# Streaming attention and a wave mixer on one core: pools and woven generators against static tiles in one listed order, with turns by DMA

## The chip, the cores and the metric

The kernel runs on one core of a Trainium2 chip. The metric is the device time of one execution in microseconds (us), here the median of three runs. The profile is one execution of the same program; its span runs from the first to the last instruction and is a little shorter than the measured time. Engines: PE multiplies matrices and writes to PSUM, DVE and ACT are the two engines that read PSUM and do elementwise work (ACT also has the table functions exp and sine), POOL works on SBUF only and issues casting DMAs, SP issues plain DMAs. Each engine carries out its instructions in program order and waits on semaphores for the others, so the order in which the program lists the work is part of its speed.

## The reference, cut to what matters

```python
# attention: B=4, H=8 heads, S=768, D=64; heads 0, 2, 6 are "retrieval", the other five "streaming"
scores = (q @ k.T) / sqrt(D)
causal = rel >= 0                                   # rel = query position - key position
stream_keep = causal & ((key < 4) | (rel < 64))     # 4 sink keys and a window of 64
mask = causal for heads 0, 2, 6; stream_keep for heads 1, 3, 4, 5, 7
a = softmax(where(mask, scores, -1e9))
x = (a @ v) laid out as (B, S, 512)

# wave mixer on x: w_tok_* are (768, 768) over tokens, w_theta and w_ch (512, 512) over channels
theta = x @ w_theta
zr, zi = x * cos(theta), x * sin(theta)
y = w_tok_r @ zr + w_tok_i @ zi                     # over tokens, per batch
u = x + y
out = u + relu(u @ w_ch)
```

All inputs and the output are float32; both kernels compute in bf16 with float32 accumulation.

## The kernel before

Work is written as Python generators that yield an estimate of their PE cost; `weave` interleaves the next batch's attention with the mix of the batch at hand. Tiles come from pools: three PSUM pools of two slots each (`ps_s` of two banks, `ps_m` and `ps_x` of one).

```python
    ps_s = ctx.enter_context(tc.tile_pool(name="ps_s", bufs=2, space=bass.MemoryType.PSUM))
    ps_m = ctx.enter_context(tc.tile_pool(name="ps_m", bufs=2, space=bass.MemoryType.PSUM))
    ps_x = ctx.enter_context(tc.tile_pool(name="ps_x", bufs=2, space=bass.MemoryType.PSUM))
    # ... (cut)
    def load_qk(b, parts=((0, 8),)):          # casting DMAs on POOL's queue; the first batch in two parts
        # ... (cut)
                nc.gpsimd.dma_start(out=state[what, b][:, sl], in_=src[:, sl])

    def transposes(b, n):                     # n: one of four pairs of heads
        # ... 12 transposes of 64x128 into pt for q and for k ...
            if what == "q" and b > 0:
                nc.scalar.copy(o, i)          # qT
            else:
                nc.vector.tensor_copy(o, i)   # kT, and the first batch's qT
        sinks(n)                              # copies the 4 sink keys of streaming heads to kS (POOL)

    def score_unit(n, banks, un):
        # retrieval heads: 128 keys against all later queries, in rows of up to 512 columns
        # streaming heads: 12 blocks of 64 keys, each against its own 64 queries and the next 64:
                for c in range(NQ):
                    lo = max(64 * c if c != 1 else 0, q0)
                    hi = min(64 * c + 128, S, q0 + w)
                    if lo < hi:
                        half = slice(64 * (c % 2), 64 * (c % 2) + 64)
                        mms[y].append((ps[half, y, lo - q0:hi - q0], kT[n][rows, c * 64:(c + 1) * 64], qT[n][rows, lo:hi]))
        # ... (cut) exp on ACT into P or P_st, masks on DVE afterwards

    def sink_scores():                        # sink keys of all five streaming heads in one product
        # ... 6 matmuls (kS, qT), then exp into p_sink

    def values(b, i):                         # 128 queries, 4 heads at a time
        for par in range(2):
            # ...
                else:
                    s = STREAM.index(h)
                    if i:
                        mms.append((av[:, g], p_sink[:, i * 128:(i + 1) * 128], vs[:, b, s]))
                    mms.append((av[:, g], P_st[:, s, 256 * i + 64:256 * i + 192], vx[:, s, i]))
                    mms.append((av[:, g], P_st[:, s, 256 * i + 128:256 * i + 256], vt[:, h, i]))
            # ...
            nc.vector.reciprocal(r, av[:, :, D])      # the 65th column of v is 1, so it holds the sum
            nc.vector.tensor_tensor(dst, av[:, :, :D], r.unsqueeze(2).to_broadcast([128, 4, D]), ALU.mult)

    def turn_x(b, i):
        pt = ps_x.tile([128, 1024], BF16, tag="x", name="pt")
        for kk in range(KD):
            nc.tensor.transpose(pt[:, kk * 128:(kk + 1) * 128], x[:, i, kk * 128:(kk + 1) * 128], ident)
        nc.vector.tensor_copy(xT[:, :, i * 128:(i + 1) * 128], pt[:, :DM].rearrange("p (k t) -> p k t", k=KD))

    def phases(b, i):                         # theta for two blocks, then
        nc.scalar.activation(ct, ps, AF.Sin, bias=half_pi)
        nc.scalar.activation(st, ps, AF.Sin)
        for y in range(2):
            nc.vector.tensor_tensor(state["zr", b][:, i + y], x[:, i + y], ct[:, y], ALU.mult)
            nc.gpsimd.tensor_tensor(state["zi", b][:, i + y], x[:, i + y], st[:, y], ALU.mult)

    def mix(b):
        def turn(t):                          # as turn_x, for u; the copy to uT is on ACT
        def channel(t):                       # 4 matmuls with w_ch, relu and add on DVE, store on SP
        # per block t of 128 tokens: 12 matmuls into py, u = x + py on DVE
    # ... (cut)
    for b in range(B):
        if b + 1 < B:
            m = mix(b)
            if b == 0:
                m = chain(token_weights(2, NB), m)    # transposes of w_tok, by PE
            weave((m, 23000), (attention(b + 1), 19000))
        else:
            drain(mix(b))
```

Of the kernel before, what the change touches and what calls it, by code (L numbers as in the profile page):

```python
# [18 lines left out]
STREAM = [1, 3, 5, 7, 4]  # L19


def drain(gen):
    for _ in gen:
        pass


def weave(*parts):

    live = [[0.0, n, g, float(total)] for n, (g, total) in enumerate(parts)]
    while live:  # L30
        live.sort(key=lambda x: (x[0] / x[3], x[1]))
        part = live[0]
        try:
            part[0] += next(part[2])
        except StopIteration:
            live.pop(0)
# [3 lines left out]
def kernel(  # L40
    ctx: ExitStack,
    tc: tile.TileContext,
    q: bass.AP,
    k: bass.AP,
    v: bass.AP,
    is_retrieval: bass.AP,
    n_sink,
    window,
    moe_w_theta: bass.AP,
    moe_w_tok_r: bass.AP,  # L50
    moe_w_tok_i: bass.AP,
    moe_w_ch: bass.AP,
    out: bass.AP,
):
    nc = tc.nc
    B, H, S, D = q.shape
    DM = H * D
    NB = S // 128
    KD = DM // 128
    n_sink = int(n_sink)  # L60
    window = int(window)
    assert window == 64 and n_sink * len(STREAM) <= 32
    NS = n_sink * len(STREAM)
    scale = 1.0 / math.sqrt(D)

    const = ctx.enter_context(tc.tile_pool(name="const", bufs=1))
    big = ctx.enter_context(tc.tile_pool(name="big", bufs=1))
    two = ctx.enter_context(tc.tile_pool(name="two", bufs=2))
    stage = ctx.enter_context(tc.tile_pool(name="stage", bufs=4))
    work = ctx.enter_context(tc.tile_pool(name="work", bufs=2))  # L70
    ps_s = ctx.enter_context(tc.tile_pool(name="ps_s", bufs=2, space=bass.MemoryType.PSUM))
    ps_m = ctx.enter_context(tc.tile_pool(name="ps_m", bufs=2, space=bass.MemoryType.PSUM))
    ps_x = ctx.enter_context(tc.tile_pool(name="ps_x", bufs=2, space=bass.MemoryType.PSUM))

    ctx.enter_context(tc.manual_schedule())


    ident = const.tile([128, 128], BF16, name="ident")
    m_causal = const.tile([128, 128], BF16, name="m_causal")
    m_stream = const.tile([128, S], BF16, name="m_stream")  # L80
    half_pi = const.tile([128, 1], F32, name="half_pi")
    w_theta_sb = const.tile([128, KD, DM], BF16, name="w_theta_sb")
    w_ch_sb = const.tile([128, KD, DM], BF16, name="w_ch_sb")
    wtokT = [const.tile([128, NB, S], BF16, name=f"wtokT{n}") for n in "ri"]

    qT = [big.tile([128, S], BF16, name=f"qT{n}") for n in range(4)]
    kT = [big.tile([128, S], BF16, name=f"kT{n}") for n in range(4)]

    kS = [big.tile([128, 128], BF16, name=f"kS{n}") for n in range(4)]
    vt = big.tile([128, H, NB, D + 1], BF16, name="vt")  # L90

    vx = big.tile([128, len(STREAM), NB, D + 1], BF16, name="vx")

    vs = big.tile([128, B, len(STREAM), D + 1], BF16, name="vs")
    p_sink = big.tile([128, S], BF16, name="p_sink")

    NQ = S // 64
    P_st = big.tile([128, len(STREAM), NQ * 128 + 64], BF16, name="P_st")

    state = {}  # L100


    def load_v(b, pairs=range(4)):
        src = v[b].rearrange("h (j p) d -> p h j d", p=128)
        for n in pairs:
            t = stage.tile([128, 2, NB, D], F32, tag="st_v", name="st_v")
            state["v", b, n] = t
            for x, h in enumerate(PAIRS[n]):
                nc.sync.dma_start(out=t[:, x], in_=src[:, h])


    def load_qk(b, parts=((0, 8),)):
        for what in "qk":
            state[what, b] = two.tile([128, H, NB * D], BF16, tag=f"{what}b", name=f"{what}b")
        for hs in parts:
            for what, a in (("q", q), ("k", k)):
                src = a[b].rearrange("h (p j) d -> p h (j d)", p=128)
                sl = slice(*hs)
                nc.gpsimd.dma_start(out=state[what, b][:, sl], in_=src[:, sl])

    def cast_v(b, n, first=False):
        t = state["v", b, n]
        h0, h1 = PAIRS[n]
        (nc.vector if first else nc.gpsimd).tensor_copy(vt[:, h0:h1 + 1:2, :, :D], t)
        for x, h in enumerate((h0, h1)):
            if not IS_RETR[h]:
                s = STREAM.index(h)
                nc.gpsimd.tensor_copy(vx[:64, s, :, :D], t[:64, x])
                nc.gpsimd.tensor_copy(vx[64:, s, 1:, :D], t[64:, x, :NB - 1])

    def sinks(n):
        for x, h in enumerate(PAIRS[n]):
            if not IS_RETR[h]:
                c = STREAM.index(h) * n_sink
                rows = slice(64 * x, 64 * x + 64)
                nc.gpsimd.tensor_copy(kS[n][rows, c:c + n_sink], kT[n][rows, :n_sink])


    def transposes(b, n):
        h0, h1 = PAIRS[n]  # L140
        for what, dst in (("q", qT), ("k", kT)):
            pt = ps_x.tile([128, 1024], BF16, tag="x", name="pt")
            for j in range(NB):
                for x, h in enumerate((h0, h1)):
                    nc.tensor.transpose(pt[64 * x:64 * x + 64, j * 128:(j + 1) * 128], state[what, b][:, h, j * D:(j + 1) * D], ident)  # L145
            o = dst[n].rearrange("d (p j) -> d p j", j=NB)
            i = pt[:, :S].rearrange("d (j p) -> d p j", j=NB)
            if what == "q" and b > 0:
                nc.scalar.copy(o, i)
            else:  # L150
                nc.vector.tensor_copy(o, i)  # L151
        sinks(n)
# [3 lines left out]
    LOW = [[(0, 0, 512)], [(1, 128, 384), (3, 384, 128)], [(2, 256, 256)]]  # L156
    HIGH = [[(0, 512, 256), (1, 512, 256)], [(2, 512, 256), (3, 512, 256)], [(4, 512, 256), (5, 640, 128)]]


    def units(n, half):  # L160
        rs, w = (LOW, (0, 512)) if half == 0 else (HIGH, (512, 256))
        h0, h1 = PAIRS[n]
        if n == 0:
            return [(n, [(0, h0, r), (1, h1, r)]) for r in rs]
        if n == 1:
            return [(n, [(1, h1, rs[0]), (0, h0, w)]), (n, [(1, h1, rs[1]), (1, h1, rs[2])])]
        return [(n, [(0, h0, w), (1, h1, w)])]

    pending = []

    def masks_now():
        while pending:
            pending.pop(0)()

    def score_unit(n, banks, un):
        ps = ps_s.tile([128, 2, 512], F32, tag="s", name="ps")
        mms = [[], []]
        width = []
        used = [sum(w for _, _, w in what) for _, _, what in banks if isinstance(what, list)]
# [72 lines left out]
        if masks:  # L252
            pending.append(causal)
# [197 lines left out]
    at = 0  # L451
# [99 lines left out]
```

The softmax here doesn't subtract the row's maximum and nothing guards it: scores larger than these inputs give would overflow.

## Time and profile before

| | us |
|---|---|
| measured, median of 3 (lowest, highest) | 258.34 (257.64, 259.43) |
| span of the profiled execution | 255.5 |
| mean granted PE clock | 0.984 |

The costliest groups, by line and tile:

```profile
L336 POOL TENSOR_TENSOR zi<-x,st 128x512 bf16<-128x512 bf16 x24 | 30.0, 1268 | 104.9 <-ACT st L333 104.9
L349 ACT COPY uT<-pt 128x512 bf16<-128x512 bf16 x24 | 14.1, 586 | 46.7 <-PE pt L347 46.7
L327 PE MATMUL ps<-w_theta_sb,xT 128*128 128x512 bf16 x89 | 24.2, 391 | 7.9 <-DVE xT L318 7.6
L368 DVE TENSOR_TENSOR u<-x,py 128x512 bf16<-128x512 bf16 x24 | 16.5, 687 | 23.8 <-PE py L364 23.8
L356 DVE SCALAR_TENSOR_TENSOR ot<-pc,u 128x512 f32<-128x512 f32 x24 | 16.5, 689 | 8.5 <-PE pc L354 7.3
```

A line reads: source line, engine, operation, output <- inputs, shapes, count; then the busy time of the group and the mean in ns of one; then how long the engine stood idle just before the instructions of the group, and what ended most of that. Idle time of an engine that is not the limit costs nothing. PE's records overlap, since matmuls are pipelined: the time that a stream of matmuls needs is the distance between their starts, not the sum of their durations.

### The profile page before, as it was taken

What the parts mean: (1) busy time and instruction counts of PE and PEld (TensorE: products, weight loads), DVE (VectorE), ACT (ScalarE), POOL (GpSimd) and SP (SyncE); (2) the same over time, 40 slices, a digit from 0 to 9 for tenths busy, and PEclk for the clock granted to TensorE, in tenths of its full rate; (3) what the DMA queues carried; (4) which work ended last, traced back from release to release, by engine and by line L of the source; (5) the groups of instructions that cost most, each with busy time, mean ns of one, the idle gap of its engine ahead of it and who ended that gap; (6) DMA issues with size and microseconds to landing.
All of it is one profiled execution on the core that took longest, in us unless ns stands there. A gap on an engine that the chain in (4) does not pass through costs nothing.

```text
span 255.5 us, 5058 instructions
## 1 busy us (share of the span) xinstructions
PE 192.3 (75%) x2095; PEld 109.5 (43%) x2124; DVE 134.8 (53%) x312; ACT 111.0 (43%) x142; POOL 84.9 (33%) x133
## 2 busy tenths in 40 slices
PE   0202659774677999889798999876989998868993
PEld 0101436642463456544444456433444564324440
DVE  6103686766443547654656387445573874442433
ACT  2002327553548764244568721636697216341010
POOL 8532168018639300031687000216940002161000
PEclk9999999999779999999999999999999999999998
DMA  7999237998235891110356960030001100300123
GB/s 133 190 194 181 65 83 132 213 166 136 37 73 114 119 187 48 45 41 0 126 124 113 190 154 30 13 123 3 0 3 41 44 22 24 123 3 0 41 82 123
DMA packets 40006, 22.61 MB, mean 88 GB/s; under 512 B 26160, under 2 KB 36912, under 8 KB 39984
## 3 DMA queue, kind: packets, MB, share of 16 engines
q0 software_dynamic: 11440, 9.71, 24.8%
q1 hardware_dynamic: 28544, 12.59, 19.0%
q8 instruction: 16, 0.26, 0.5%
q14 instruction: 6, 0.05, 0.1%
HBM read 25.71 MB, written 6.29 MB: 125 GB/s over the span
## 4 chain that ended last, share of the span: by engine, by line
PE 47%; ACT 16%; DVE 13%; issue 11%; DMA 6%; POOL 4%; POOLq 1%; DVEq 0%; ACTq 0%
PE py L364 19%; PE ps L209 7%; PE pav L306 5%; ACT P L229 5%; DMA kb<-in_k_dram 5%; PE ps L327 4%; ACT ct L332 4%; PE pc L354 4%; DVE kT L151 3%; PE pt L145 3%; DVE zr L335 3%; DVE ot L356 2%; DVE x L310 2%; POOL zi L336 2%; PE ps L277 2%
## 5 line engine op out<-in xcount | busy, mean ns | idle before, releaser
L336 POOL TENSOR_TENSOR zi<-x,st 128x512 bf16<-128x512 bf16 x24 | 30.0, 1268 | 104.9 <-ACT st L333 104.9
L209 PE MATMUL ps<-qT,kT 64*64 64x128 bf16 (+6 forms) x380 | 25.6, 256 | 21.5 <-DVE kT L151 16.8
L364 PE MATMUL py<-zi,wtokTi 128*128 128x512 bf16 x137 | 37.8, 379 | 1.7 <-POOL zi L336 1.4
L364 PE MATMUL py<-zr,wtokTr 128*128 128x512 bf16 x130 | 36.6, 380 | 1.7 <-issue 0.8
L349 ACT COPY uT<-pt 128x512 bf16<-128x512 bf16 x24 | 14.1, 586 | 46.7 <-PE pt L347 46.7
L229 ACT ACTIVATE P<-ps 128x1024 bf16<-128x1024 f32 (+2 forms) x24 | 20.9, 919 | 23.5 <-PE ps L209 23.4
L335 DVE TENSOR_TENSOR zr<-x,ct 128x512 bf16<-128x512 bf16 x24 | 17.3, 763 | 25.9 <-ACT ct L332 25.9
L327 PE MATMUL ps<-w_theta_sb,xT 128*128 128x512 bf16 x89 | 24.2, 391 | 7.9 <-DVE xT L318 7.6
L368 DVE TENSOR_TENSOR u<-x,py 128x512 bf16<-128x512 bf16 x24 | 16.5, 687 | 23.8 <-PE py L364 23.8
L209 PEld LDWEIGHTS <-kT 64*64 64x64 bf16 (+1 forms) x380 | 12.7, 108 | 37.3 <-DVE kT L151 17.8
L332 ACT ACTIVATE ct<-ps,half_pi 128x1024 f32<-128x1024 f32 x12 | 13.4, 1114 | 25.7 <-PE ps L327 17.3
L354 PE MATMUL pc<-w_ch_sb,uT 128*128 128x512 bf16 x96 | 24.2, 379 | 0.0
L310 DVE TENSOR_TENSOR x<-pav,r 128x256 bf16<-128x256 f32 x48 | 20.4, 425 | 1.7
L356 DVE SCALAR_TENSOR_TENSOR ot<-pc,u 128x512 f32<-128x512 f32 x24 | 16.5, 689 | 8.5 <-PE pc L354 7.3
L151 DVE COPY kT<-pt 128x768 bf16<-128x768 bf16 x16 | 15.3, 954 | 8.9 <-PE pt L145 6.6
L364 PEld LDWEIGHTS <-wtokTi 128*128 128x128 bf16 x144 | 12.9, 98 | 13.3 <-issue 1.6
L225 ACT ACTIVATE P_st<-ps 128x1024 bf16<-128x1024 f32 (+1 forms) x16 | 12.8, 810 | 13.3 <-PE ps L209 13.3
L145 PE MATMUL pt<-ident,qb 128*64 128x128 bf16 x192 | 10.2, 255 | 9.8 <-DMA qb<-in_q_dram 7.7
L364 PEld LDWEIGHTS <-wtokTr 128*128 128x128 bf16 x144 | 11.9, 97 | 12.9 <-issue 2.4
L327 PEld LDWEIGHTS <-xT 128*128 128x128 bf16 x96 | 8.8, 99 | 17.9 <-DVE xT L318 9.5
L306 PE MATMUL pav<-vs,p_sink 128*128 128x65 bf16 x100 | 13.3, 195 | 3.5 <-ACT wtokTr L386 1.8
L306 PE MATMUL pav<-vx,P_st 128*128 128x65 bf16 x120 | 15.7, 196 | 0.0
(70 smaller groups left out, 319.1 us busy)
## 6 DMA issues: line engine op xcount, KB each, us to landing
st_v<-in_v_dram SPq DMA_DIRECT2D x32, 192.0 KB, 3.1
out_dram<-ot SPq DMA_DIRECT2D x24, 256.0 KB, 2.0
qb<-in_q_dram POOLq DMA_DIRECT2D x3, 768.0 KB, 10.2
kb<-in_k_dram POOLq DMA_DIRECT2D x3, 768.0 KB, 13.1
wtok<-in_moe_w_tok_r_dram POOLq DMA_DIRECT2D x3, 384.0 KB, 5.0
wtok<-in_moe_w_tok_i_dram POOLq DMA_DIRECT2D x3, 384.0 KB, 6.8
w_theta_sb<-in_moe_w_theta_dram POOLq DMA_DIRECT2D x1, 512.0 KB, 15.1
w_ch_sb<-in_moe_w_ch_dram POOLq DMA_DIRECT2D x1, 512.0 KB, 6.8
```

The costliest lines, as they stand in the source:

```text
L151: nc.vector.tensor_copy(o, i)
L209: nc.tensor.matmul(o, l, r, start=True, stop=True, skip_group_check=True)
L229: nc.scalar.activation(P.rearrange("p (y c) -> p y c", y=2), ps[:, :, :w0], AF.Exp, scale=scale)
L306: nc.tensor.matmul(o, l, r, start=(m == 0), stop=True, skip_group_check=True)
L310: nc.vector.tensor_tensor(dst, av[:, :, :D], r.unsqueeze(2).to_broadcast([128, 4, D]), ALU.mult)
L327: nc.tensor.matmul(ps[:, y], xT[:, kk, (i + y) * 128:(i + y + 1) * 128], w_theta_sb[:, kk], start=(kk == 0), stop=(kk == KD - 1))
L332: nc.scalar.activation(ct, ps, AF.Sin, bias=half_pi)
L335: nc.vector.tensor_tensor(state["zr", b][:, i + y], x[:, i + y], ct[:, y], ALU.mult)
L336: nc.gpsimd.tensor_tensor(state["zi", b][:, i + y], x[:, i + y], st[:, y], ALU.mult)
L354: nc.tensor.matmul(pc, uT[t][:, kk], w_ch_sb[:, kk], start=(kk == 0), stop=(kk == KD - 1))
L356: nc.vector.scalar_tensor_tensor(ot, pc, 0.0, u[t], ALU.max, ALU.add)
L364: nc.tensor.matmul(py, w[:, s, t * 128:(t + 1) * 128], z[:, s], start=(n == 0), stop=(n == len(order) - 1))
```

## The change

The kernel is rewritten around the same arithmetic. It is meant to take work off PE and to put all work in an order chosen as a whole.

- All tiles are static: 8 PSUM banks addressed by number, u and uT in six buffers, the output in four. There are no generators. One list, `ORDER`, names every step of every engine with batch, block, PSUM bank and, where there is a choice, the engine (A, D or P).
- A streaming head now has, for each block of 128 queries, its own 128 keys (slot D) and a second block of 128 columns that holds the sink keys and the 64 keys before (slot O, keys copied to `kO`, values to `vo`). The separate sink scores and the `vx` copies go; two value products a block in place of three.
- x and u are turned by transposing DMAs from SBUF to SBUF (`xd`, `ud`), except the first batch's x and the very last u, which PE still turns (`xp`, `up`).
- The first batch's q and k arrive as float32 by plain DMAs, pair by pair, and are cast on chip. q and k of later batches go to single buffers. zi is shared between DVE and POOL; zr is done for two blocks at once; one norm serves both halves of a block.

The core of the diff (cut):

```diff
-STREAM = [1, 3, 5, 7, 4]
+SLOTS = [("D", 0)] + [(w, i) for i in range(1, 6) for w in "DO"]
+ST_W = 128 * len(SLOTS)
+ORDER = """
+lf.q.0 lf.k.0 lf.q.1 lf.k.1 lf.q.2 lf.k.2 lf.q.3 lf.k.3 cf.q.0.A lv.0.0 tq.0.q.0.0 lv.0.1 cf.k.0.A lv.0.2 eq.0.q.0.0.A lv.0.3 tq.0.k.0.1 cf.q.1.P
 ... (cut: about 60 such lines)
+u.3.3.2 mx.3.4.2.0 ud.3.3 mx.3.5.2.1 u.3.4.0 ch.3.0.2 ud.3.4 u.3.5.1 ch.3.2.0 o.3.0.2 up.3.5.1 st.3.0 o.3.2.0 ch.3.3.2 ue.3.5.1.A st.3.2 ch.3.5.3
+o.3.3.2 ch.3.4.0 st.3.3 o.3.5.3 st.3.5 o.3.4.0 st.3.4
+"""
-    ps_s = ctx.enter_context(tc.tile_pool(name="ps_s", bufs=2, space=bass.MemoryType.PSUM))
+    banks = [psum.tile([128, 2, 512], F32, name=f"bank{n}") for n in range(4)]
+    def load_first(what, n):
+        nc.sync.dma_start(out=t[:, n], in_=a[0, h0:h1 + 1:2].rearrange("h (p j) d -> p h (j d)", p=128))
+    def sink_keys(b, n, eng):
+        copy(eng, kO[n][r, :, 64:], kT[n][r].rearrange("d (i g s) -> d i g s", g=2, s=64)[:, :NB - 1, 1])
+        copy(eng, kO[n][r, :, :n_sink], kT[n][r, :n_sink].unsqueeze(1).to_broadcast([r.stop, NB - 1, n_sink]))
-    def sink_scores():
+                    if kind == "D":
+                        keys = kT[n][r, i * 128:(i + 1) * 128]
+                    else:
+                        keys = kO[n][r, i - 1]
+                    mms.append((o[:, c:c + 128], keys, qT[n][r, i * 128:(i + 1) * 128]))
-                    if i:
-                        mms.append((av[:, g], p_sink[:, i * 128:(i + 1) * 128], vs[:, b, s]))
-                    mms.append((av[:, g], P_st[:, s, 256 * i + 64:256 * i + 192], vx[:, s, i]))
-                    mms.append((av[:, g], P_st[:, s, 256 * i + 128:256 * i + 256], vt[:, h, i]))
+                    mms.append((o, at_stream(h, 128 * SLOTS.index(("D", i)), 128), vt[:, i, s]))
+                    if i:
+                        mms.append((o, at_stream(h, 128 * SLOTS.index(("O", i)), 128), vo[:, i - 1, s - 2]))
+    def turn(o, t):
+        nc.sync.dma_start_transpose(out=o, in_=t)
+        "xd": lambda b, i: turn(xT[int(b) % 2][:, :, int(i) * 128:(int(i) + 1) * 128], x[int(b) % 2][:, int(i)]),
+        "ud": lambda b, t: turn(uT[ui(int(b), int(t))], u[ui(int(b), int(t))]),
+    for step in ORDER.split():
+        name, *args = step.split(".")
+        run[name](*args)
```

The short names in the list: `s`, `e`, `m` are scores, exp and mask of a unit; `av`, `n` value products and norm; `th`, `tr`, `z` theta, sines and phases; `mx`, `u` a third of the mix of a block and the add; `ch`, `o`, `st` channel product, finish and store; `tq`/`eq` q and k transposes and their copies; `wt`/`we` those of the token weights; `l*` loads; `cf`, `cv` casts; `bv`, `sv`, `ko` the copies for `vo` and `kO`.

## The prediction

> **What bounds the kernel now.** I read the busy table first, then the slices, then the stages one by one, then the pace of single matmuls in the timeline, and last the chain.
>
> ```profile
> PE 192.3 (75%) x2095; PEld 109.5 (43%) x2124; DVE 134.8 (53%) x312; ACT 111.0 (43%) x142; POOL 84.9 (33%) x133
> ...
> PE   0202659774677999889798999876989998868993
> DMA  7999237998235891110356960030001100300123
> ...
> PE 47%; ACT 16%; DVE 13%; issue 11%; DMA 6%; POOL 4%; POOLq 1%; DVEq 0%; ACTq 0%
> ```
>
> No engine is full: TensorE (PE) is busy 75% and carries less than half of the chain that ended last; the rest of that chain is hand-overs between engines. The first 23 us have almost no PE work while the DMA row is at 9. The stages (boundaries chosen by me: the first copy out of PSUM, the first sine, the second batch's first k copy, then the k copies of the third and fourth batch, then the last sines):
>
> ```profile
> 0.00:21.30 21.30, 1.70 (x24) 1.22 (x24) 5.51 (x19) 1.28 (x1) 12.36 (x26) 1.00 1.10 176
> 21.30:53.00 31.70, 22.68 (x325) 15.23 (x328) 21.74 (x55) 14.57 (x19) 10.27 (x19) 1.00 0.74 134
> 53.00:68.70 15.70, 8.65 (x99) 5.44 (x99) 8.05 (x14) 8.10 (x9) 8.86 (x8) 0.89 0.73 113
> 68.70:126.00 57.30, 50.02 (x554) 29.06 (x563) 31.12 (x75) 29.76 (x39) 17.78 (x28) 0.97 0.39 79
> 126.00:177.20 51.20, 43.85 (x505) 24.65 (x513) 29.86 (x71) 26.94 (x35) 17.35 (x28) 1.00 0.46 99
> 177.20:228.50 51.30, 44.37 (x486) 24.57 (x494) 30.28 (x71) 26.87 (x35) 16.13 (x26) 1.00 0.09 32
> 228.50:255.50 27.00, 21.05 (x109) 9.38 (x110) 8.28 (x12) 3.51 (x6) 2.12 (x2) 0.97 0.15 58
> ```
>
> Columns: stretch, length, busy PE, PE weight load, DVE, ACT, POOL. So 68.7 us pass with one batch's attention alone, three periods of some 51 us hold a mix beside the next batch's attention, and 27 us of mix stand alone at the end.
>
> PE busy overstates PE's need. What one matmul really takes is the distance between starts:
>
> ```profile
> 147.49 0.79 PE L209 MATMUL ps<-qT,kT 64*128 64x256 bf16 x14
> 148.21 0.60 PE L364 MATMUL py<-zr,wtokTr 128*128 128x512 bf16 x2
> 148.65 0.59 PE L364 MATMUL py<-zi,wtokTi 128*128 128x512 bf16 x2
> 149.09 1.03 PE L354 MATMUL pc<-w_ch_sb,uT 128*128 128x512 bf16 x4
> 149.95 0.39 PE L317 MATMUL pt<-ident,x 128*128 128x128 bf16 x4
> 150.17 0.35 PE L306 MATMUL pav<-vt,P 128*128 128x65 bf16 x6
> 150.36 0.19 PE L306 MATMUL pav<-vs,p_sink 128*128 128x65 bf16 x1
> ```
>
> From start to next start: 256-wide scores (148.21-147.49)/14 = 51 ns; 512-wide products (149.95-149.09)/4 = 215 ns; transposes (150.17-149.95)/4 = 55 ns; value products (150.36-150.17)/6 = 32 ns. A further pace, from the chain: 24 q/k transposes in 0.79 us, 33 ns.
>
> One middle period by these: mix 72, channel 24 and theta 24 products, 120 x 0.215 = 25.8; values 148 x 0.032 = 4.7; q/k transposes 96 x 0.033 = 3.2; x and u turns 48 x 0.055 = 2.6; scores of full heads 8,064 columns and of streaming heads about 7,700, at 51 ns per 256, 3.1; sink scores 0.8. Sum 40.2 us of 51.2: PE really works 79% of the time. The whole kernel, four batches plus 72 token-weight transposes (4.0), needs about 165 us of 255.5. The gap of 90 us is waiting, and order decides it.
>
> **What the Trainium skill says.** "Perfetto Trace Analysis", Identifying the Most-Contended Engine: matmul busy share is a poor measure of headroom since matmuls are pipelined. The trace agrees: 43.85 us busy against 40.2 by pace, in a period with weight loads busy only 24.65. "TensorE: Matmul & The Clock Gate", Part 3: matmuls on different row groups run concurrently. It agrees: two half-height 256-wide scores take 2 x 51 ns, one full 256-wide at the 512-wide pace would take 107. "Advanced Engine Details and Errata", X-Bar Transpose (TRN2): transposing DMAs are as fast as regular ones, with 350-400 GB/s expected. No run here shows a transposing DMA yet. "DMA: Bandwidth & Descriptors", Anatomy of one DMA: a fixed cost of some 2 us [...]. The 256 KB stores here land 2.0 us after issue, and the 192 KB v loads 3.1. For a turn of 128 KB I take 2 to 3 us, an estimate from these two.
>
> **The change on PE.** Removed: 164 of the 192 x/u transposes (28 stay: the first batch's x and one last u), 164 x 0.055 = 9.0; 120 of 592 value products, x 0.032 = 3.8; 24 sink scores, 3.2. Streaming scores go from about 30,700 columns in 260 small matmuls to 220 x 128 = 28,160, at two at once about -0.5. First-batch q/k transposes become 48 of 128x128 in place of 96 paired ones: -0.6. Sum about -17: 165 becomes 148 us. A middle period needs 40.2-0.8-1.0-2.6 = 35.8.
>
> **The other engines.** ACT: uT copies go (24 x 0.586 = 14.1). Exps grow, since each streaming head now has 11 blocks of 128 columns, 1,408 instead of 768 plus sinks: per batch 11 units of 1024 (1.02), 4 of 768 (0.82), one of 512 (0.61) and one of 256 (0.39) = 15.5, so 62 against 53. 19 q/k copies instead of 12 at 0.80, +5.6; v, vo, x and token copies about +12. Sum 111 becomes about 130.
> DVE: the xT copies go (24 x 0.418 = 10.0; one stays); norm once for both halves, 24 x (0.19+0.69) = 21 against 28.9; stream masks 15 or so of 1024 (0.72) and 20 smaller, 21 against 12; 12 of the 24 zi products arrive from POOL at 0.69 = 8.3; zr in twos about 1.2 each = 14 against 17; v casts +5; some q/k copies leave. Sum about 140 against 135.
> POOL: zi halves (30 to 15), per-pair v copies (30) become vo and kO copies of about 14: 85 becomes about 52. DMA gets 41 turns of 128 KB, 5 MB on top of 22.6, in the part where its row was at 0 to 3.
>
> **The sum in time.** Start: q and k of pair 0 now come as 384 KB float pieces on the SP queue. At the 176 GB/s of the first stage a piece is 2.2 us; with 2 us fixed and a start at 1.3, q0 is there at 5.5, k0 at 7.7, and the last of eight at about 19-21. First scores about 10 instead of 23. From there the first batch is bound by ACT: casts 2.4, q/k copies 10 x 0.8 = 8, exps 15.5, v/x copies 4.5, sines 6.4, two table loads 2.6, one token copy 0.8 = 40 us. From 5.5 with 3-5 us of gaps for the late pieces this ends near 50, and the first mix product, which needs only the first third of the sines, starts near 46. Before, the first one in the chain is at 83.
> Of the 148 us of PE work some 21 lie before that (q/k 2.6+3, scores 3.2, values 3.6, x turns 1.3, theta 5.2, seven token turns 2.3); 127 remain. Which share of the time will PE work? Before: 79%. After: DVE needs (140-36 in the first batch)=104 and ACT about 90 us in the same stretch, so neither is the bound, and all steps sit in one list with buffers assigned, so slots no longer open and close by pool order. I choose 86%: 127/0.86 = 148. Then the last channel, finish and store, 0.9+0.7+2.0, 4 us. 46+148+4 = 198 of span; the measured time was 2.8 above the span: 200.8, say 200.
>
> **The rivals.** *Transposes by DMA as a new wait.* In the list, the PE work between a turn's issue and the product that reads it is mostly 3 to 9 us, but 2.6 to 4 us for the last two batches and 1.3 to 1.8 at two spots. At 2.5 us landing this hides; at 5 us some 20 turns would stick out by 1 to 2 us, and since stores and v loads share the SP queue in order, one late step holds the next: +20 to 35, time 220 to 235. For it: no trace shows one. Against: the list keeps the distance, and keeps PE for the very last u and the first batch, as a list would that knows what a turn costs.
> *DVE becomes the bound.* About 33 us per period against 35.8 on PE, with both orders fixed: at 80-85% DVE, PE would be near 80% again: 127/0.8 = 159, time 211.
> *The start is bound by loads.* q, k as floats, v, theta, token weights and the next batch's q, k: 13.5 MB read by about 50 us. The first four slices (25.5 us) wrote 4.5 MB by the GB/s row and read about 7.3 MB of float for it (casting loads read twice what they write), 290 GB/s, so 47 us would do, just. If it does not, mix starts at 55 instead of 46: 209.
> *The order is better than I think*, PE at 92%: 127/0.92 = 138, time 190.
>
> **Range and chances.** The optimistic case 190 less 3, the two middle rivals 209-211 plus a little of the first: 187 to 217. For less than 2% gain the waits would have to give back over 50 us of a 58 us gain; only a serial transpose path could. Faster 0.94, within 2% 0.03, slower 0.03.
>
> **What would show it.** First score near 10, first mix product near 46, middle periods near 42, PE busy near 165-170 with 60 fewer us of span. Turns in the DMA list at 2-3 us to landing; PE's wait on xT and uT under 5 us in all. Wrong if turns land at 5 us or more and head the waits of PE, if DVE shows over 85% in the middle, or if PE waits on q/k or token weights after 30 us.

## The result: 209.9 us, and where the gain came from

The changed kernel takes 209.94 us (median of 4 runs, 208.89 to 210.94) against 258.75 for the kernel before beside it: ratio 0.814, 95% interval 0.809 to 0.819. The prediction said 200, range 187 to 217.

The page of the changed kernel, to be laid beside the same rows of before (busy time by engine, 40 slices, the chain that ended last):

```profile
PE 170.2 (82%) x1707; PEld 94.0 (45%) x1728; DVE 137.7 (66%) x255; ACT 123.7 (59%) x147; POOL 55.8 (27%) x80
...
PE   0466689787879698998999779979998997899871
...
PEclk9999658999999999999999999999999999999998
DMA  5998999979859977869999304841043266013144
...
PE 46%; DVE 20%; DMA 12%; ACT 12%; issue 5%; SPq 2%; POOL 0%; DVEq 0%; ACTq 0%; POOLq 0%
```

PE gets to work sooner: before has 0 to 2 tenths in its first four slices, after has 4 in the second and 6 or more from the third to the last but one. By the busy row, PE's work falls by 22.1 us and the rest of the span by 25.4 (63.2 to 37.8). Since busy PE overstates the need, I also counted by pace: the distance from the start of each product to the next start, less what a product of its form needs. Of what is left over, stretches above 0.1 us hold some 78 us in before and 47 in after. So some 32 us of the gain are waiting that is gone, and about 16 are PE work that is gone: the two parts that the prediction counted. DMA's share of the chain has doubled, from 6% to 12%; experiment 2 asks whether that is a real bound.

Three marks cut both spans into the same parts:

| | before | after | difference |
|---|---|---|---|
| start to first score matmul | 23.1 | 10.1 | -13.0 |
| first score to first mix product | 55.7 (78.8) | 39.8 (49.9) | -15.9 |
| first mix product to the end | 176.7 (255.5) | 158.1 (208.0) | -18.6 |

In brackets the time of the mark. (The prediction put the first mix product of before at 83, which is the first one in the chain; the first in the trace starts at 78.8.)

The stages of after, with boundaries of mine, near the first score, the first batch's theta, the second batch's scores, its theta, the scores of the third and of the fourth batch, and the end of the last sines. Columns as before: stretch, length, busy PE, PE weight load, DVE, ACT, POOL, then granted clock, DMA share, GB/s.

```profile
0.00:10.10 10.10, 2.40 (x20) 1.77 (x22) 3.77 (x12) 5.18 (x6) 3.25 (x11) 1.00 0.79 264
10.10:40.00 29.90, 22.66 (x340) 17.66 (x341) 22.56 (x51) 24.41 (x34) 12.04 (x20) 0.83 1.14 200
40.00:46.90 6.90, 6.12 (x68) 4.09 (x69) 2.82 (x6) 6.11 (x7) 4.19 (x6) 1.00 0.72 99
46.90:86.00 39.10, 32.78 (x389) 18.22 (x394) 28.16 (x53) 28.18 (x37) 10.82 (x17) 1.00 0.87 163
86.00:98.00 12.00, 11.30 (x80) 5.24 (x79) 10.00 (x14) 8.18 (x9) 9.09 (x11) 1.00 0.86 197
98.00:140.00 42.00, 36.75 (x398) 19.83 (x403) 30.55 (x55) 25.53 (x30) 9.58 (x13) 1.00 0.78 136
140.00:182.00 42.00, 38.53 (x334) 18.91 (x338) 28.65 (x51) 25.54 (x28) 6.80 (x4) 1.00 0.32 73
182.00:208.00 26.00, 19.67 (x90) 8.32 (x89) 11.16 (x17) 0.59 (x1) 0.00 (x0) 0.97 0.32 100
```

In the middle no engine is full: DVE is busy 31 of 42 us, ACT 26. In 10 to 40 us ACT is busiest with 24.4 of 29.9, and the granted clock is only 0.83. The last row, 26 us of mix with nothing beside it, is as long as before's 27: the change touches little there.

The DMA list of after (KB of one, median us from issue to landing):

```profile
st_v<-in_v_dram SPq DMA_DIRECT2D x24, 256.0 KB, 4.7
out_dram<-ot SPq DMA_DIRECT2D x24, 256.0 KB, 2.2
...
uT<-u SPq DMA_TRANSPOSE x23, 2.7
early<-early SPq DMA_TRANSPOSE x12, 2.5
xT<-x SPq DMA_TRANSPOSE x6, 2.5
```

A turn lands 2.5 us after issue, as assumed. ("early" is the tile that x, its turned form and others share at different times.) But look at the queue that issues them. From the timeline of after (start, duration, then who; SPq is SP's DMA queue, PE is TensorE):

```profile
90.47 7.28 SPq L211 DMA_DIRECT2D st_v<-in_v_dram  x5
97.84 7.59 SPq L375 DMA_TRANSPOSE uT<-u  x1
105.56 0.97 SPq L432 DMA_DIRECT2D out_dram<-ot  x2
107.06 9.62 SPq L375 DMA_TRANSPOSE uT<-u  x5
...
113.70 1.04 PE L426 MATMUL bank<-w_ch_sb,uT 128*128 128x512 bf16 x4 [0.20 <-DMA uT<-u]
```

An undisturbed turn holds the queue for 1.2 us, where a store of twice its size holds it for as little as 0.33; the turn behind five v loads holds it for 7.6. Undisturbed turns in a row are issued every 1.3 us (at 167.84, 169.17 and 170.47 us in after), some 100 GB/s for 128 KB each; no run here shows the 350 to 400 GB/s that the prediction quotes.

The piece from 107.06 to 113.70 is in the chain of after as 6.6 us of DMA. Yet PE, which the piece ends on, stood idle for it only 0.20 us: it had other listed work. A chain follows what released the last step; it doesn't say that anything was idle meanwhile.

### The profile page after: what moved, and what is told of

Same layout as the page of the kernel before. It is cut to its first block, busy times and chain, and to the rows that moved or that the text cites. A ratio compares the mean times of both kernels' runs of the same rounds, so it can differ in the third digit from the quotient of the medians.

```text
span 208.0 us, 4245 instructions
## 1 busy us (share of the span) xinstructions
PE 170.2 (82%) x1707; PEld 94.0 (45%) x1728; DVE 137.7 (66%) x255; ACT 123.7 (59%) x147; POOL 55.8 (27%) x80
## 4 chain that ended last, share of the span: by engine, by line
PE 46%; DVE 20%; DMA 12%; ACT 12%; issue 5%; SPq 2%; POOL 0%; DVEq 0%; ACTq 0%; POOLq 0%
PE bank L416 19%; DMA uT<-u 8%; PE bank L426 8%; ACT P L306 5%; PE bank L363 5%; DVE u L422 4%; PE bank L276 4%; PE bank L399 4%; DMA early<-in_q_dram 3%; DVE ot L429 3%; PE bank L232 3%; DVE kT L238 2%; DVE zr L411 2%; DVE early L411 2%; ACT kT L236 2%
## 5 line engine op out<-in xcount | busy, mean ns | idle before, releaser
L306 ACT ACTIVATE P<-bank 128x1024 bf16<-128x1024 f32 (+2 forms) x64 | 57.3, 948 | 15.5 <-PE bank L276 15.5
L426 PE MATMUL bank<-w_ch_sb,uT 128*128 128x512 bf16 x91 | 23.8, 379 | 5.6 <-DMA uT<-u 1.8
L416 PE MATMUL bank<-zr,wtokTr 128*128 128x512 bf16 x67 | 25.5, 381 | 3.5 <-DVE zr L411 1.1
L328 DVE TENSOR_TENSOR P<-P,m_stream 128x1024 bf16<-128x1024 bf16 (+3 forms) x36 | 21.0, 587 | 10.1 <-ACT P L306 9.8
L416 PE MATMUL bank<-early,wtokTi 128*128 128x512 bf16 x71 | 26.9, 379 | 0.3 <-issue 0.2
L276 PE MATMUL bank<-qT,kT 64*128 64x128 bf16 (+3 forms) x240 | 23.0, 271 | 4.7 <-DVE kT L238 1.7
L416 PE MATMUL bank<-early,wtokTr 128*128 128x512 bf16 x68 | 25.7, 379 | 1.1 <-ACT qT L236 0.4
L416 PE MATMUL bank<-zi,wtokTi 128*128 128x512 bf16 x69 | 26.1, 379 | 0.5 <-issue 0.3
L363 PEld LDWEIGHTS <-P 128*128 128x128 bf16 x472 | 17.2, 101 | 3.2 <-ACT P L306 0.4
L363 PE MATMUL bank<-vt,P 128*128 128x65 bf16 x372 | 17.8, 198 | 0.0
L238 POOL COPY kO<-kT 128x320 bf16<-128x320 bf16 (+3 forms) x18 | 7.9, 466 | 26.8 <-DVE kT L238 23.1
## 6 DMA issues: line engine op xcount, KB each, us to landing
wtok<-in_moe_w_tok_r_dram POOLq DMA_DIRECT2D x6, 192.0 KB, 10.4
wtok<-in_moe_w_tok_i_dram POOLq DMA_DIRECT2D x6, 192.0 KB, 10.4
```

Source lines behind the costliest of these rows:

```text
L238: (nc.vector if eng == "D" else nc.gpsimd).tensor_copy(o, i)
L276: nc.tensor.matmul(*mms[g], start=True, stop=True, skip_group_check=True)
L306: nc.scalar.activation(o, two(bank)[:, :, :o.shape[2]], AF.Exp, scale=scale)
L328: nc.vector.tensor_tensor(o, o, mk, ALU.mult)
L363: nc.tensor.matmul(o, l, r, start=(m == 0), stop=True, skip_group_check=True)
L416: nc.tensor.matmul(one(bank), wtokT[n][:, s, t * 128:(t + 1) * 128], z[b % 2][:, s], start=(s == 0 and n == 0), stop=(s == NB - 1 and n == ...
```

## The experiments

Where an edit moves steps of the list, the names are those of the change: `s` scores, `ud`/`xd` turns by DMA, `up`/`xp` turns by PE with the copy `ue`/`xe`, `lv` loads of v, `z` the products zr and zi, the last number a PSUM bank, a letter the engine. Medians in us; ratios are to the kernel before on the same chip.

### 1. The turns back on PE, in the new list; the turns by DMA, in the old kernel

The first puts all 41 turns back on PE (a turn's transposes into a bank that is free at that place, and a copy), the second does only the DMA turns in the kernel before.

```diff
 after, pe_turns
-u.0.0.0 e.1.8.4 ud.0.0 s.1.7.6          ... xd.1.0 mx.0.5.2.2
+u.0.0.0 e.1.8.4 s.1.7.6 ... up.0.0.1 ue.0.0.1.A    ... xp.1.0.0 xe.1.0.0.D
 before, before_dma_turns
-            nc.tensor.transpose(pt[...], x[:, i, ...], ident)      # and the copy; the same for u
+        nc.sync.dma_start_transpose(out=xT[:, :, i * 128:(i + 1) * 128], in_=x[:, i])
```

> The changed kernel, but all 41 turns by DMA go back to PE transposes with a copy on DVE (x) or ACT (u), in free banks near the old places. Theory (work taken off PE counts, since PE is busy some 82% of the time after the start): 164 transposes x 0.055 = 9 us on PE, plus 18 copies of 0.42 on DVE and 23 of 0.59 on ACT as new hand-overs: 218 to 224 us. Rival (the order hides turns either way, and the DMA turns give nothing): 209 to 212. Rival (waits for the DMA turns, 4.3 us on PE, are as dear as the transposes): 206 to 209.

> The kernel before, with only x and u turned by DMA (all 48). Theory (without a list that leaves 2.5 to 4 us between a turn and its reader, the landing takes the place of the copy it removes: the last x block of each batch is turned right before theta reads it): PE loses 10.6 us of work and gains waits, so 248 to 256 us against 258.7. Rival (DMA turns carry the gain of the change): 240 us or less. Rival (landing hits hard in this order): 262 or more.

Measured: 231.48 (0.895, interval 0.887 to 0.902), 7 us above what the theory allowed, and 283.79 (1.098, 1.090 to 1.107), the second rival. Turns by DMA save 21.5 us in the list and cost 24.4 in the old kernel. The two are not quite alike: the list leaves the first batch's x and the last u on PE, so it has 41 turns by DMA against 48. In the old kernel the waits show the loss (engine, line, whom it waited for; us in total, times, longest):

```profile
PE ps L324 <- DMA xT<-x: 21.5, 7, 13.7
PE pc L348 <- DMA uT<-u: 19.2, 6, 5.2
```

Its turns land in 2.4 to 2.5 us by the median too. But a generator asks for a turn just before the product that reads it, and turns that were issued beside the loads of the next batch landed 9 to 10 us after issue. The longest wait, 13.7 us, comes from the queue itself. SP's queue and PE in this kernel:

```profile
41.38 6.14 SPq L315 DMA_TRANSPOSE xT<-x  x3
47.58 20.02 SPq L109 DMA_DIRECT2D st_v<-in_v_dram  x8
67.70 5.78 SPq L315 DMA_TRANSPOSE xT<-x  x3
...
72.85 4.39 PE L324 MATMUL ps<-w_theta_sb,xT 128*128 128x512 bf16 x12 [13.74 <-DMA xT<-x]
```

The fourth block of the first batch's x is complete at 47.7, but eight loads of v hold the queue until 67.6, and theta waits for the turn behind them. The first mix product then starts at 92.5 in place of 78.8, which is more than half of the loss; and the list does not turn this batch's x by DMA at all. What the old kernel would lose with only the list's 41 turns, or with its turns ahead of the loads, no run tells. In the list, PE waits only 4.3 us for all its turns together:

```profile
PE bank L426 <- DMA uT<-u: 1.8, 4, 0.6
...
PE bank L399 <- DMA xT<-x: 1.3, 2, 1.0
PE bank L399 <- DMA early<-early: 1.2, 1, 1.2
```

Of the 21.5 us that the list loses without DMA turns, 9.0 can be put down to the PE work itself (41 turns of four transposes at 55 ns). Waits for the neighbour of a PSUM bank, explained in experiment 3, grow from 8.3 to 14.3 us, since 41 more results need banks: 6.0. The other 6.5 I could not assign.

### 2. The loads of v, later

The piece of the chain shown above suggests freeing the SP queue: here the six loads of the fourth batch's v come after the second batch's turns.

```diff
-xd.1.5 sv.2.P o.0.3.4 th.1.0.0 cv.2.2.D lv.3.1 st.0.3 lv.3.5 bv.2.2.P mx.0.4.2.5 lv.3.0 ...
+xd.1.5 sv.2.P o.0.3.4 th.1.0.0 cv.2.2.D st.0.3 bv.2.2.P mx.0.4.2.5 ...
+m.2.8 ud.1.3 lv.3.1 lv.3.5 lv.3.0 lv.3.2 lv.3.3 lv.3.4 ...
```

> The changed kernel with the six v loads of the last batch moved behind the u turns of the second batch on the SP queue; they had kept one turn 7.6 us in issue and the next 6.6 us to landing. Theory (PE stood idle only 0.2 us for that turn, since its list had other work until 113 us): 208.5 to 211, no change that counts. Rival (the chain shows 6.6 us of landing there, so the queue is the bound): 203 to 206.

Measured: 209.06 (0.808, 0.802 to 0.814) against 209.94, which is nothing that counts, as the executions of the two overlap. The 6.6 us of DMA in the chain were no bound, as the 0.20 us of idle PE had said.

### 3. The order alone, and the PSUM tiles

The same steps of after, on the same engines, with the same DMA turns, in an order woven as in the kernel before: one batch's mix block by block, with scores, values and turns of the next between.

```diff
-... cf.q.0.A lv.0.0 tq.0.q.0.0 lv.0.1 cf.k.0.A lv.0.2 eq.0.q.0.0.A ...
+... mx.0.2.0.4 av.1.0.0 n.1.0.0 ud.0.1 mx.0.2.1.4 s.1.12.2 e.1.12.2 s.1.13.0 ... mx.0.2.2.4 u.0.2.4 ... ch.0.0.5 o.0.0.5
```

> The same steps on the same engines as the changed kernel, with the same static tiles and DMA turns, but listed in the way of the kernel before: generators of attention and mix woven by their PE cost, scores in two bank pairs, mix and channel in two banks, transposes in two. Theory (the order is the largest single part after the early start): middle periods at 79% PE use in place of 83%, with the start losing 5 to 15 us more to the stage by stage order: 224 to 240 us. Rival (work removed, early loads and static tiles make the gain, and the order little): 209 to 215.

Measured: 347.28 (1.341, 1.331 to 1.351), over 100 us beyond what had been expected. The timeline of this kernel at its end, DVE and PE, shows the cause:

```profile
320.24 0.69 DVE L422 TENSOR_TENSOR u<-early,bank 128x512 bf16<-128x512 bf16 x1 [2.84 <-PE bank L416]
320.99 1.02 PE L426 MATMUL bank<-w_ch_sb,uT 128*128 128x512 bf16 x4 [0.78 <-DVE u L422]
...
322.05 0.69 DVE L429 SCALAR_TENSOR_TENSOR ot<-bank,u 128x512 f32<-128x512 f32 x1 [1.11 <-PE bank L426]
...
322.79 0.38 PE L416 MATMUL bank<-early,wtokTr 128*128 128x512 bf16 x1 [0.78 <-DVE ot L429]
```

The channel product (320.99) reads a uT that has been ready for a while, and writes bank 5. It waits for DVE's u, which reads bank 4. The next mix product (322.79) writes bank 4 and waits for `ot`, which reads bank 5. Neither needs the other. But the 8 banks are four tiles of two, and the waits are kept by tile: a product into one bank waits for the readers of both. The woven order had put mix and channel into the two halves of one tile, so they went in lock-step. Matching each step of the list to its instruction, I counted the time for which PE stood idle for a reader of the other half while its own bank had long been free: 64.1 us here, and 8.3 us in after, at 17 places. (The count depends on what "long" means: with every such wait counted in full it is 77 and 10 us.) Two of these in after's timeline:

```profile
120.82 1.02 PE L426 MATMUL bank<-w_ch_sb,uT 128*128 128x512 bf16 x3 [0.55 <-DVE kT L238]
...
124.78 1.02 PE L426 MATMUL bank<-w_ch_sb,uT 128*128 128x512 bf16 x4 [0.84 <-DVE kT L238]
```

A channel product has nothing to do with a copy of kT; that copy reads the bank next door.

The Trainium skill, "PSUM — Partial Sum Buffer", in "PSUM bank collisions raise a hardware error", says to guard PSUM with semaphores by bank and quadrant, by bank being the simple version. So the coarser wait comes from how the tiles are declared, not from the memory, and the two tests that follow agree: with waits by single banks the same work goes faster. One splits the upper four banks of the woven kernel into tiles of their own:

```diff
-    banks = [psum.tile([128, 2, 512], F32, name=f"bank{n}") for n in range(4)]
+    banks = [psum.tile([128, 2, 512], F32, name=f"bank{n}") for n in range(2)]
+    singles = [psum.tile([128, 512], F32, name=f"single{n}") for n in range(4)]
```

> The woven order of the run before it (347 us), unchanged, but with the four banks that mix, channel and transposes use as four tiles of one bank instead of two tiles of two. Theory (a good part of that loss was the shared tile: PE idle 64 us until a reader of the neighbour bank was done): 255 to 285 us, and a granted clock back above 0.9. Rival (the order as such is that bad): 320 or more.

Measured: 284.84 (1.093, 1.086 to 1.101), 62.4 us less than with shared tiles, though the clock stayed at 0.86 to 0.90. The other test leaves after's list and order alone and changes only bank numbers (152 of 203 uses), so that neighbours are in use at different times:

```diff
-lv.0.3 tq.0.k.0.1 cf.q.1.P lv.0.4 eq.0.k.0.1.A lv.0.5 tq.0.q.1.0 cf.k.1.A s.0.0.2 eq.0.q.1.0.D
+lv.0.3 tq.0.k.0.2 cf.q.1.P lv.0.4 eq.0.k.0.2.A lv.0.5 tq.0.q.1.1 cf.k.1.A s.0.0.6 eq.0.q.1.1.D
```

> The changed kernel with the same steps in the same order, and only the PSUM bank numbers chosen anew. Two banks form one tile, and in the trace PE stands idle 8.3 us until a reader of the other bank of the tile is done, though its own bank had long been free; the new numbers keep such neighbours apart where the list allows. Theory (these waits are a real cost): half of them go, and as much again on DVE and ACT: 203 to 207 us. Rival (another operand is always about to be late, so the wait only changes its name): 208.5 to 211.

Measured: 205.84 (205.14 to 206.33; 0.791, 0.787 to 0.795), 4.1 us below after. The count of neighbour waits falls from 8.3 to 0.9 us (in full, from 10.4 to 1.7), so about half of what was removed came out of the time. Page of this kernel:

```profile
PE 171.3 (84%) x1728; PEld 94.9 (47%) x1728; DVE 141.6 (70%) x255; ACT 123.4 (61%) x147; POOL 57.3 (28%) x80
...
PE   0476689987879689997899987989999998699991
...
PEclk9999999999999999999999999999999999999998
```

The clock row is full here and wasn't in after. That isn't the gain: other runs of the same kernel with a mean clock of 0.97, that of after, had spans of 203.1 to 204.1, those of after at 0.97 had 206.8 to 208.0.

### 4. zr before zi

The twelve zr products (1024 wide, on DVE) take 1.21 us at best, but 1.8 and 1.6 in the mean of their two groups. From the timeline of after:

```profile
95.66 1.21 POOL L411 TENSOR_TENSOR early<-early,st 128x512 bf16<-128x512 bf16 x1
95.76 2.19 DVE L411 TENSOR_TENSOR early<-early,ct 128x1024 bf16<-128x1024 bf16 x1
```

POOL's zi starts first and ends at 96.87; from there to the end of zr, 97.95, is 1.08 us, nearly what a zr takes alone. The Trainium skill, "SBUF — State Buffer", "Who interferes with whom", says that a DVE instruction with two SBUF inputs contends with a GpSimd instruction that reads SBUF, and that the order of issue decides who blocks. That predicts a cure that removes no work: list zr ahead of both zi, so that PE's first mix product has its input first.

```diff
-z.1.1.i.1.D z.1.1.i.0.P mx.1.0.0.1 tr.1.2.4 z.1.1.r.2.D s.2.7.2
+z.1.1.r.2.D z.1.1.i.1.D z.1.1.i.0.P mx.1.0.0.1 tr.1.2.4 s.2.7.2
```

> The changed kernel with the zr product of each two blocks listed ahead of the two zi products. Six of the twelve zr take 1.6 to 2.4 us and the others 1.2; the long ones are those that begin while POOL multiplies zi. Theory (the two engines hinder each other, and zr lies ahead of the first mix products of a batch): long zr fall to 1.2 to 1.5, and 1 to 4 us go: 206 to 209. Rival (DVE has slack there, PE has other work): 209 to 211.

Measured: 208.66 (208.30 to 209.48; 0.803, 0.799 to 0.807), 1.3 less than after. That is at the edge of the noise: the executions of the two overlap, the intervals of their ratios do not. The timeline of this kernel at the third batch, DVE and POOL:

```profile
135.05 1.22 DVE L411 TENSOR_TENSOR zr<-x,ct 128x1024 bf16<-128x1024 bf16 x1
...
135.60 1.68 POOL L411 TENSOR_TENSOR zi<-x,st 128x512 bf16<-128x512 bf16 x1 [2.18 <-ACT st L404]
...
136.18 1.65 DVE L411 TENSOR_TENSOR zi<-x,st 128x512 bf16<-128x512 bf16 x1
```

Now zr keeps its 1.22 us. POOL's zi starts inside it and takes 1.68, against about 1.2 alone; DVE's next product takes 1.65, against 0.68, because POOL is at work by then. Ten of twelve zr are at most 1.23 us. DVE's time for zr and zi together stays as it was, 27.6 us against 27.8. The waiting has moved to those that nobody needs first, which is all the gain there is.

### 5. The first loads: float pieces or casting pieces

Is it the float load that brings the first score forward? Here the first batch's q and k come pair by pair by casting DMAs on POOL's queue, without the float tiles and the casts on chip. (The edit also turns the first batch's q and k in 96 small transposes in place of 48, as for later batches, and sets up the constants after these loads.)

```diff
-lf.q.0 lf.k.0 lf.q.1 lf.k.1 ... cf.q.0.A lv.0.0 tq.0.q.0.0 lv.0.1 cf.k.0.A
+lc.q.0 lc.k.0 lc.q.1 lc.k.1 ... lv.0.0 tq.0.q.0.0 lv.0.1
```

> The changed kernel, with the first batch's q and k loaded pair by pair by casting DMAs on POOL's queue instead of float loads and casts on chip. Theory (what pulls the start is that a pair is a piece of its own, not the float form; the cast on chip costs what the queue saves): 208 to 214 us, first score at 9 to 12 us. Rival (the plain queue is what makes the start): first score at 14 or later and 215 to 222 us.

Measured: 209.89 (0.807, 0.802 to 0.812), first score at 12.1, first mix product at 51.5. The form of the load is worth 2 us at the first score and nothing at the end. That leaves the cut into pairs and the order of the queue, which no run tests by themselves. An early first score is not enough either: the woven kernel with split tiles has its first score at 7.6 us, and its first mix product at 79.8, where the kernel before had it.

### 6. The woven order with PE turns

This completes a square: woven or listed order, PE or DMA turns, on the same steps. The edit puts the turns of weave_split on PE as in experiment 1.

```diff
-s.1.7.2 e.1.7.2 m.1.4 m.1.5 ud.0.0 mx.0.1.1.5 ...
+(the same with up.0.0 and ue.0.0 in place of ud.0.0, and so for all x and u)
```

> The woven order with tiles of one bank (284.8 us), but with all turns on PE as in the kernel before. It completes a square: order woven or listed, turns by PE or by DMA. Theory (turns by DMA need an order that leaves room; in the kernel before they cost 25 us, in the list they save 21): 252 to 268 us, so that the turns by DMA cost the woven order 17 us or more. Rival (static tiles and streaming blocks do not suit the woven order, turns or not): 278 or more.

Measured: 275.41 (1.070, 1.059 to 1.080), between the two theories.

| | PE turns | DMA turns |
|---|---|---|
| woven (split tiles) | 275.4 | 284.8 |
| listed | 231.5 | 209.9 |
| the kernel before | 258.8 | 283.8 |

(The last row has 48 turns by DMA, the others 41.) Two things are in it. Against my woven order the list is worth 43.9 us with PE turns and 74.9 with DMA turns, more than any other part that was tested, and that with waits by pairs of banks still in the list and mostly gone from the woven kernels. And DMA turns cost time in both woven kernels: in weave_split PE stood idle 16.0 us for uT alone. Of the three orders tried, turns by DMA pay in the one made for them.

Without its list the new kernel is slower than the old one, 275.4 to 258.8, in spite of some 8 us less PE work for attention. I didn't find out why. My woven order takes two tiles in turn for scores, and its PE stood idle 19.3 us for the exps that read them; how it would do with a better hand I can't say.

### 7. Every turn issued twice

How much slack do the turns have? Each is issued once into a tile that nobody reads, and then into its place. The second comes 1.25 to 1.9 us later than the only one did, and the queue is held twice as long.

```diff
+        nc.sync.dma_start_transpose(out=spare, in_=t)
         nc.sync.dma_start_transpose(out=..., in_=t)
```

> The changed kernel with each of its 41 turns issued twice, first into a tile that nobody reads, then into its place: the turn lands about 1.2 us later, in a burst of six more. Theory (the first rival of the prediction: the list leaves 2.6 to 4 us for the last two batches, so a landing of 3.7 or more sticks out): some 20 turns by up to 1.2 us and the bursts more, 216 to 230 us. Rival (other work hides it): 209 to 212.

Measured: 258.20 (0.997, 0.992 to 1.002): 48 us more, the whole gain gone, and 28 us above what the theory allowed. Waits of PE and ACT in this kernel:

```profile
ACT ct L406 <- PE bank L402: 27.9, 4, 12.8
...
PE bank L402 <- DMA early<-early: 22.5, 8, 9.5
...
PE bank L429 <- DMA uT<-u: 10.2, 5, 4.5
...
PE bank L402 <- DMA xT<-x: 3.7, 3, 2.1
```

PE's waits for turns grow from 4.3 to 36.4 us. Theta waited up to 9.5 us for its last turn in the second batch and 4.2 in the fourth. On SP's queue at the first of these places:

```profile
98.00 1.96 SPq L378 DMA_TRANSPOSE early<-early  x1
101.07 1.55 SPq L377 DMA_TRANSPOSE spare<-early  x1
102.67 1.34 SPq L378 DMA_TRANSPOSE early<-early  x1
104.06 0.57 SPq L211 DMA_DIRECT2D st_v<-in_v_dram  x1
104.73 4.19 SPq L435 DMA_DIRECT2D out_dram<-ot  x1
```

Turns issued at 101 to 103 us landed 9 to 10 us later, beside loads. And in a burst the delays add up: from the first to the last of a batch's six x turns the queue needs 18.1 us in the third batch and 20.4 in the fourth, against 9.9 and 10.0 in after. So this run doubles two things that can't be separated by it, the time on the queue and the traffic (writes to the spare tile also wait for each other). What it shows is that the order has no room for turns that take twice the queue.

### 8. The corrections together

`best` has rebank, zr_first and v3_late; `best_act` also moves three casts or copies of v and one k cast of the first batch from ACT to POOL.

```diff
-cf.k.1.A ... bv.0.0.A ... bv.0.1.A ... cv.0.5.A
+cf.k.1.P ... bv.0.0.P ... bv.0.1.P ... cv.0.5.P
```

> The changed kernel with three things that each helped or did no harm: new bank numbers (205.8), zr ahead of zi (208.7), the last v loads behind the u turns (209.1). Theory (they lie at different places, so their gains of 4.1, 1.3 and 0.9 add up): 203 to 204.5 us. Rival (they shorten the same waits): 205 to 206.

> As the run named best, with four copies and casts of the first batch moved from ACT to POOL (two copies into vo, one cast of v, one of k: some 2.5 us of ACT). Theory (the prediction: the first batch is bound by ACT): 1 to 2.5 us less than best. Rival (by then loads, DVE and PE take turns as the last one): within 0.7 us of best.

Measured: 204.28 (202.58 to 205.38; 0.792, 0.782 to 0.802) and 203.93 (203.70 to 204.68; 0.792, 0.786 to 0.797). Two of the six executions of `best`, the profiled one among them, ran at a lower clock than the rest (0.95 against 0.97) and are left out. By the medians `best` is where its theory put it, and best_act is 0.4 us below it, as its rival said. Against rebank's 205.84 that is 1.6 and 1.9 us less, but `best` and best_act ran on another chip than rebank, and the ratios of all three lie within each other's intervals. All three beat both kernels; which of them is best these runs don't tell, so what zr_first and v3_late add to rebank isn't shown. The first mix product of best_act starts at 47.2, 1.5 earlier than rebank's 48.7, which speaks for ACT as the limit of the start, but weakly, since zr ahead of zi is in it too.

## Why the prediction was right, and two terms that were mis-sized

**Where the gain comes from: right.** About 16 us of PE work, 17 predicted, and the rest waiting. DVE 138 of 140 predicted, POOL 56 of 52, PE 170 of 165 to 170. ACT has 124 of 130, but there the prediction added wrongly: its terms, 111 - 14.1 + 9 + 5.6 + 12, make 123.5. DVE's terms, too, make some 136 and not 140, before the copies that leave without a figure.

**First score near 10: right,** 10.1, though two errors offset each other. The first q and k landed at 4.1 and 5.2 us, not at 5.5 and 7.7, and the first kT was there at 8.5; but the list has the transposes of the next pair's q ahead of the first score, and PE waited 1.7 us for their cast on POOL.

**First mix product near 46: 49.9, 4 us off.** ACT was the busiest engine of that stretch as the prediction said (24.4 of 29.9 us between 10 and 40), but its gaps were taken at 3 to 5 us, and between 5 and 50 it stood idle 9.7 us. The woven kernel shows how much depends on order here: earlier first score, first mix product 30 us later.

**127 us of PE work at 86%: the step that was mis-sized.** The work itself was right: in rebank's trace, which lacks no product, the paces give 21.4 us before the first mix product and 126.6 from there on, against 21 and 127. The share was not: from 49.9 to 204, the tail of 4 taken off the span, are 154 us and not 148: 127/154 = 82%. These 6 us and the 4 before make the 10 by which 200 was too low. Behind them are two waits that the prediction didn't have. It read "slots no longer open and close by pool order" as if a bank number were a slot; the slots are tiles of two banks, and PE waits 8.3 us for readers next door. Changing the numbers alone gave 4.1 us back. And it put zr in twos at "about 1.2 each"; beside POOL's zi it is up to 2.4, and the order that avoids it for zr gave 1.3 back. By one trace each, from the first mix product on rebank is 3.1 us shorter than after and zr_first 1.1, together 4.2 of the 6 us; before it they win 1.2 and 0.7 of the 4. That the two gains add no run shows cleanly, and what the rest is stays open.

**Middle periods near 42: right in the mean only.** From theta to theta 45.0 and 38.1 us for the two later ones (131.8 less 86.8, 169.9 less 131.8).

**Turns land in 2 to 3 us, PE waits under 5: right,** 2.5 and 4.3. The estimate from stores and v loads held: 2.5 us for 128 KB, beside 2.2 for a 256 KB store in the same run. (The 2 us of fixed cost in the prediction are, by the section that it cites of the Trainium skill, "DMA: Bandwidth & Descriptors", Anatomy of one DMA, a fit for DMAs issued by POOL; the turns are issued by SP.) What the prediction didn't have is the 1.2 us that each holds the queue, some 50 us of SP's time for 41 turns.

**Rival 1, turns as a new wait: rightly set aside, wrongly sized.** Landing at 5 us was put at 220 to 235. Turns of which each comes 1.3 to 1.9 us later at its issue, and the last of a burst some 8 to 10, cost 48 us and gave 258. I counted only turns that would stick out one by one. A late turn delays theta, theta the sines, these the whole next mix, and loads in the queue behind it.

**Rivals 2 and 3** (DVE as the bound, start bound by loads): the time, 209.9, is near what each of them gave, 211 and 209, but neither is the reason. DVE is busy 31 of 42 us in the middle, and PE's longest waits name other things. Of the start, slower loads are excluded only in part: start_cast had its first score 2 us later and the same end, and after 14 us neither PE nor ACT waits for a load in after's trace, but POOL's casts still do, for 2.4 us. Nor did the last sign of being wrong appear: after 30 us PE waits for no load of q, k or token weights.

**What stays open:** how the list's 75 us over the woven order divide. 29.9 lie before the first mix product (79.8 to 49.9), 45 behind it, but in weave_split the mean granted clock is 0.88 against 0.97, so a part of those may be the slower clock and not waiting.

## What to carry to other kernels

A transfer that takes the place of engine work pays only where the order leaves room for its landing and for its place in the queue: test it in the order that it will live in, since the same 41 turns saved 21 us in one order and cost 9 in another, and in the old kernel one turn behind eight loads cost over 13. Before a step in the chain is called a bound, look at how long the engine behind it stood idle; 6.6 us in the chain were 0.2 us of idle. And look for waits that name a reader with no business there, such as a channel product that waits for a copy of k: they are tiles that share a guard, and a renumbering removes them without touching the work.

## What the runs showed of the hardware that was not expected

- A transposing DMA of 128 KB between two places of SBUF holds SP's queue for 1.19 to 1.23 us and lands 2.4 to 2.5 us after issue when nothing disturbs it; behind five 256 KB v loads it held the queue for 7.6 us, and the slowest landing was 12.1.
- Elementwise products of two SBUF inputs on DVE and POOL at once delay one of the two, nearly always the one that starts second: DVE 1024 wide from 1.21 to up to 2.41 us, 512 wide from 0.68 to 1.66; POOL 512 wide from about 1.2 to up to 2.04.
- The granted clock is lower in kernels whose PE is idle more, though not in strict order: mean 0.82 in weave_order (PE idle for 35% of the span), 0.88 to 0.90 in weave_split, turns_twice and before_dma_turns (27 to 31%), 0.94 in weave_pe (26%), but 0.98 in before (25%), 0.97 in after (18%), and 0.97 to 1.00 in runs of rebank (16%). What causes it no run was made to tell.
